# Scaling from PSUM at the start-up, with the scan and the decay moved to later places, in a fused state-space and gated feed-forward kernel

## Chip, cores, metric

One core of a Trainium2 chip. The metric is the device time of one execution in microseconds (us); lower is better. TensorE is called PE, VectorE DVE, ScalarE ACT and GpSimd POOL in the profile.

On one core "slow" means only this: more than 1.5% above the fastest execution of the same kernel. A ratio is the mean time of one kernel's fast runs over that of the other's fast runs of the same rounds, so it is not quite the ratio of the medians that are quoted. The experiments ran in four batches, on four different chips; kernels of different batches are compared through their ratio to the kernel before.

## The reference

A chunked state-space layer (4 batches, 8 heads, 768 tokens, head size 32, state size 16) feeds a gated feed-forward layer (256 to 1536 and back, on 3072 tokens):

```python
cum = np.cumsum(log_a_chunk, axis=-1)
L = np.exp(cum[..., :, None] - cum[..., None, :]) * causal
y_intra = einsum('bhij,bhjd->bhid', einsum('bhin,bhjn->bhij', C, B) * L, x)
y_inter = einsum('bhin,bhnd->bhid', C, state) * np.exp(cum)[..., None]
state   = exp(sum(log_a_chunk)) * state + sum_j(B_j x_j * exp(cum_end - cum_j))
...
out = (np.maximum(x @ w_gate, 0) * (x @ w_val)) @ w_out
```

The kernel never takes a logarithm: it forms the running product of `a` with a scan, multiplies C by it and B by its inverse. The tokens are handled in twelve pairs of chunks. Batch 0 holds pairs 0 to 2 and has its own scan (`cp0`); a long scan (`cp`) serves batches 1 to 3.

The names that the views use: `BT` and `CT` are the scaled and transposed B and C of a pair, g their product, `gs` the masked copy of g; inter multiplies C by the carried state, D multiplies `gs` by x, and both add up y, copied as `yT`. A gate/value group (`gv`) is the four matmuls that make gate and value for 128 features of 256 tokens; h is the value times the gate after its ReLU. The groups after the first are called late groups here. The decay matmuls make the factors of batches 1 to 3 from the long scan and from `pick`, a scaled selection matrix. g and the groups take their PSUM buffers from the same five banks. A warm-up is a matmul on zeros whose result nobody uses.

## The kernel before

The start-up, in program order on each engine (cuts marked):

```python
keep_warm(22)                       # 128x128 matmuls on zeros, result unused
d = factors()                       # 4 fp32 matmuls: cp0, transposed, into PSUM
decays(0)
keep_warm(8)
nc.vector.tensor_copy(wfac[:, 1], d)
nc.vector.memset(wg[0:1, 0, 0:1], 0.0)      # the first weights wait for this
weights(0, 2); weights(2, 4); weights(4, 6, (0,))      # issued by POOL
scale_wide(0, 1, V)                 # C of pair 0
nc.vector.reciprocal(wfac[:, 0, :, :, 0], wfac[:, 1, :, :, 0])
scale_wide(0, 0, V)                 # B of pair 0
transp(0, 1, False); keep_warm(4); transp(0, 0, True)
tevac(0, A_, V)
nc.vector.reciprocal(wfac[:, 0, :, :, 1:3], wfac[:, 1, :, :, 1:3])
scan(0, H)                          # the long scan
scale_wide(1, 1, P_); scale_wide(1, 0, P_); weights(4, 6, (1,))
keep_warm(6)
G_wide(0); keep_warm(7); gcopy(0, 0); gmask(0, 2, V, True); keep_warm(5, ...)
...
f0 = gvh(0, 0, 0, True)             # first gate/value group of 256 tokens
G_wide(1)
decay()                             # fp32 matmuls for batches 1 to 3
adds(1)
...
late = [gvh(0, f, 0, True) for f in (1, 2, 3)]
...
decay_factors()
...
halves(0, 1, 0, 1, 2, 3, 4, 5)
```

## Time and profile before

| | before |
|---|---|
| time, median of the first 3 runs | 124.55 us (124.37 to 124.59) |
| span of the profiled execution | 122.7 us |
| PE busy | 118.1 us, 96% |
| PE full from | 10.57 us |

The views that carry the argument on the chain are in the prediction. One more: the timeline of PE in its first 7 us. Its columns are start us, length us of the group, engine, line, operation, output and inputs, array part, and how many.

```profile
1.06 2.53 PE L189 MATMUL w<-warm 128*128 128x128 bf16 x22 [1.06 <-DVE tmask L163]
3.52 0.63 PE L217 MATMUL fac<-identf,cp 48*64 48x24 f32 x8
4.08 1.03 PE L189 MATMUL w<-warm 128*128 128x128 bf16 x8
...
5.17 0.62 PE L189 MATMUL w<-warm 128*128 128x128 bf16 x4
...
5.79 0.50 PE L189 MATMUL w<-warm 128*128 128x128 bf16 x6
6.42 0.42 PE L418 MATMUL g<-CT,BT 32*64 32x256 bf16 x16
```

See the length of a group against its count: 22 warm-ups in 2.53 us are one per 0.11 us, 6 warm-ups from 5.79 on take 0.50 us in all, with one every 0.06. From about 5.7 us PE runs at twice the rate. The slower spacing is called half rate below, the faster one full rate.

### The profile page before, as it was taken

To read this page: it belongs to the slowest core of one execution; us is meant where nothing else is said; L and a number is where in the kernel's file an instruction comes from. 1 tells how busy PE (TensorE), PEld (TensorE's weight loads), DVE (VectorE), ACT (ScalarE), POOL (GpSimd) and SP (SyncE) were. 2 spreads that over 40 slices of the span, in tenths; PEclk is the share of its full clock that TensorE was granted. 3 is DMA by queue.
4 is the path that set the end of the run, shared out by engine and by line. 5 is a ranking of instruction groups with operands and counts; after the bars stand their busy time and mean duration, and the time that the engine had idled before them with its cause. 6 is when DMAs were issued, how large, how long until landed. Compare 5 with 4: busy or idle time off the path is not lost.

```text
span 122.7 us, 3665 instructions
## 1 busy us (share of the span) xinstructions
PE 118.1 (96%) x1404; PEld 82.4 (67%) x1404; DVE 88.0 (72%) x200; ACT 76.3 (62%) x169; POOL 48.2 (39%) x108
## 2 busy tenths in 40 slices
PE   6989999999999999999999999999999999999990
PEld 6856784577875478874577864677854678844790
DVE  4798988872799864988763897855987656788410
ACT  0467688835987725786635886545877447876420
POOL 6499989361455127360351806033600033000000
DMA  3999999996979995999999498960580002200022
GB/s 63 220 208 146 171 192 194 189 172 103 115 89 139 143 142 143 103 150 205 150 114 140 154 136 138 110 117 0 189 52 0 0 0 91 85 0 0 0 91 86
DMA packets 77489, 13.93 MB, mean 113 GB/s; under 512 B 70064, under 2 KB 77472, under 8 KB 77472
## 3 DMA queue, kind: packets, MB, share of 16 engines
q1 hardware_dynamic: 70128, 10.61, 54.2%
q0 software_dynamic: 4288, 2.36, 14.1%
q10 hardware_dynamic: 3056, 0.72, 2.7%
q8 instruction: 11, 0.18, 0.6%
q14 instruction: 6, 0.05, 0.1%
HBM read 11.13 MB, written 3.15 MB: 116 GB/s over the span
## 4 chain that ended last, share of the span: by engine, by line
PE 92%; POOL 4%; DVE 1%; issue 1%; DVEq 0%
PE o L713 26%; PE gv L686 21%; PE gate L668 15%; PE val L671 15%; PE y L643 2%; PE g L548 2%; PE w L189 2%; POOL wg L199 2%; POOL bs L322 1%; PE y L632 1%; PE o L707 1%; PE A_ps L601 1%; PE g L418 1%; POOL wv L199 1%; PE y L523 1%; PE dec L262 1%
## 5 line engine op out<-in xcount | busy, mean ns | idle before, releaser
L675 DVE TENSOR_TENSOR h<-r,val 128x512 bf16<-128x512 bf16 x44 | 30.0, 685 | 7.3 <-ACT r L674 7.2
L713 PE MATMUL o<-wo,h 128*128 128x256 bf16 x276 | 33.1, 273 | 0.0
L674 ACT ACTIVATE r<-gate 128x512 bf16<-128x512 f32 x44 | 26.3, 597 | 9.7 <-PE gate L668 9.3
L713 PEld LDWEIGHTS <-h 128*128 128x128 bf16 x276 | 25.9, 98 | 5.3 <-issue 1.7
L668 PE MATMUL gate<-yT,wg 128*128 128x512 bf16 x88 | 26.2, 379 | 0.0
L671 PE MATMUL val<-yT,wv 128*128 128x512 bf16 x88 | 26.2, 379 | 0.0
L692 DVE TENSOR_TENSOR h<-r,gv 128x256 bf16<-128x256 bf16 x56 | 22.5, 419 | 2.6 <-ACT r L689 1.8
L689 ACT ACTIVATE r<-gv 128x256 bf16<-128x256 f32 x56 | 21.2, 386 | 2.3 <-PE gv L686 0.2
L686 PE MATMUL gv<-yT,wg 128*128 128x256 bf16 x112 | 21.5, 273 | 0.0
L686 PE MATMUL gv<-yT,wv 128*128 128x256 bf16 x112 | 21.4, 273 | 0.0
L556 POOL TENSOR_SCALAR_AFFINE_SELECT gs<-gs 128x512 bf16<-128x512 bf16 (+1 forms) x16 | 8.0, 523 | 30.0 <-ACT gs L567 30.0
L573 DVE TENSOR_TENSOR gs<-g,maskUT 128x512 bf16<-128x512 f32 x16 | 10.3, 685 | 11.4 <-issue 5.6
L338 POOL TENSOR_TENSOR tok<-bcr,scaleBC 128x128 bf16<-128x128 f32 x32 | 12.2, 409 | 14.1 <-DMA bcr<-in_B_dram 13.0
L671 PEld LDWEIGHTS <-wv 128*128 128x128 bf16 x88 | 8.6, 98 | 10.4
L668 PEld LDWEIGHTS <-wg 128*128 128x128 bf16 x88 | 8.6, 98 | 8.9
L686 PEld LDWEIGHTS <-wv 128*128 128x128 bf16 x112 | 11.0, 98 | 1.3
L686 PEld LDWEIGHTS <-wg 128*128 128x128 bf16 x112 | 10.2, 98 | 1.9 <-DVE yT L536 0.2
L567 ACT CAST gs<-g 128x512 bf16<-128x512 f32 x8 | 4.7, 589 | 6.7 <-PE g L548 6.7
L656 ACT CAST yT<-y 128x512 bf16<-128x512 f32 x8 | 4.7, 586 | 5.1 <-PE y L643 2.5
L433 DVE TENSOR_TENSOR gs<-g,wmask 128x512 bf16<-128x512 f32 x9 | 5.9, 680 | 2.6 <-PE g L418 2.6
L189 PE MATMUL w<-warm 128*128 128x128 bf16 x49 | 5.5, 284 | 1.1 <-DVE tmask L163 1.1
L189 PEld LDWEIGHTS <-warm 128*128 128x128 bf16 x58 | 5.0, 126 | 1.7 <-DVE tmask L163 1.1
(122 smaller groups left out, 115.8 us busy)
## 6 DMA issues: line engine op xcount, KB each, us to landing
xr<-in_x_dram SPq DMA_DIRECT2D x17, 128.0 KB, 3.2
out_dram<-ob SPq DMA_DIRECT2D x3, 512.0 KB, 3.2
bcr<-in_C_dram SPq DMA_DIRECT2D x17, 64.0 KB, 2.9
bcr<-in_B_dram SPq DMA_DIRECT2D x17, 64.0 KB, 2.9
out_dram<-ob SPq DMA_DIRECT2D x4, 256.0 KB, 3.5
xr<-in_x_dram SPq DMA_DIRECT2D x3, 256.0 KB, 4.1
wo<-in_moe_w_out_dram POOLq DMA_DIRECT2D x2, 384.0 KB, 8.5
wg<-in_moe_w_gate_dram POOLq DMA_DIRECT2D x4, 128.0 KB, 4.0
```

The costliest lines, as they stand in the source:

```text
L189: nc.tensor.matmul(out=w, lhsT=warm, rhs=rhs, start=True, stop=True)
L338: eng.tensor_tensor(out=dst[:, t, j * (1 + t)], in0=src[:, j, :, t], in1=f[:, j, :, 4 * t:4 * t + 4].to_broadcast([128, 2, 4, N]), op=ALU. ...
L556: nc.gpsimd.affine_select(out=dst, in_=dst, pattern=[[0, n], [1, 128]], compare_op=ALU.is_ge, fill=0.0, base=0, channel_multiplier=-1)
L573: nc.vector.tensor_tensor(out=d[:, q], in0=g[q], in1=m, op=ALU.mult)
L668: nc.tensor.matmul(out=g, lhsT=wg[:, k, fs], rhs=yT[:, k, tk], start=(k == 0), stop=(k == 1))
L671: nc.tensor.matmul(out=v, lhsT=wv[:, k, fs], rhs=yT[:, k, tk], start=(k == 0), stop=(k == 1))
L674: nc.scalar.activation(r, g, AF.Relu)
L675: nc.vector.tensor_tensor(out=fst[b][:, f], in0=r, in1=v, op=ALU.mult)
L686: nc.tensor.matmul(out=gv_[:, j], lhsT=w[:, k, fs], rhs=yT[:, k, tk], start=(k == 0), stop=(k == 1), skip_group_check=True)
L689: nc.scalar.activation(r, gv_[:, 0], AF.Relu)
L692: nc.vector.tensor_tensor(out=fst[b][:, f, u * 256:(u + 1) * 256], in0=r, in1=gv_[:, 1], op=ALU.mult)
L713: nc.tensor.matmul(out=o[:, ts % 2], lhsT=fst[b][:, f, ts * 128:(ts + 1) * 128], rhs=wo[:, f], start=(f == 0), stop=(f == NF - 1), skip_gr ...
```

## The change

The intent: take the copy and the two reciprocals of the factors, and the long scan, out of the chain of pair 0, so that PE becomes full sooner. The inverse is taken of the scan itself, and a second set of factor matmuls brings it into PSUM, from where DVE scales. ACT makes the SBUF copies from which POOL scales the later pairs. The long scan runs in two halves in gaps of DVE, so the decay matmuls, which need it, move to a later place. The second warm-up group, eight matmuls, goes, and the others lose two each.

```diff
     load_bc(0, 0, nc.sync, nc.scalar)
+    load_x(0, nc.sync, nc.scalar)
+    load_bc(1, 1, nc.sync)
     a_sb = glob.tile([2 * BH, H], FP32)
@@ 
-    nc.vector.tensor_copy(heads, ...)
+    rc0 = glob.tile([R, 128], FP32)
+    nc.vector.reciprocal(rc0, cp0)
@@ scale_wide
-        f = wfac[:, j, :, :, p]
+        f = (fac[j] if p == 0 else wfac[:, j])[:, :, :, p]
@@ the start-up
-    keep_warm(22)
-    d = factors()
-    decays(0)
-    keep_warm(8)
-    nc.vector.tensor_copy(wfac[:, 1], d)
+    keep_warm(20)
+    fac = [None, factors(cp0)]
+    fac[0] = factors(rc0)
@@
     scale_wide(0, 1, V)
-    nc.vector.reciprocal(wfac[:, 0, :, :, 0], wfac[:, 1, :, :, 0])
+    nc.scalar.copy(out=wfac[:, 1], in_=fac[1])
     scale_wide(0, 0, V)
+    nc.scalar.copy(out=wfac[:, 0], in_=fac[0])
     transp(0, 1, False)
-    keep_warm(4)
+    keep_warm(2)
@@
-    nc.vector.reciprocal(wfac[:, 0, :, :, 1:3], wfac[:, 1, :, :, 1:3])
-    scan(0, H)
+    chunk_heads()
+    decays(0)
@@
-    keep_warm(6)
+    keep_warm(4)
@@
-    middle()
+    scan(0, H // 2)
@@
     yevac_wide(0, A_, V)
+    scan(H // 2, H)
     load_bc(2, 1, nc.sync)
@@
     cast_x(1, V)
+    middle(0)
+    middle(1)                       # pick, now on POOL
@@
     G_wide(1)
-    decay()
     adds(1)
@@
-    decay_factors()
@@
-    halves(0, 1, 0, 1, 2, 3, 4, 5)
+    halves(0, 1, 0, 1, 2)
+    decay()
+    halves(0, 1, 3)
+    decay_factors()
+    halves(0, 1, 4, 5)
```

(The two loads at the top are moved up: they stood below the load of `a_sb`. Left out: the function bodies that take an argument more, and the decay matmuls that leave out batch 0, 48 columns in place of 64.)

More of the change, by code (lines that the diff above doesn't have):

```diff
@@ L138 @@
     load_bc(0, 0, nc.sync, nc.scalar)
+    load_x(0, nc.sync, nc.scalar)
+    load_bc(1, 1, nc.sync)
     a_sb = glob.tile([2 * BH, H], FP32)
     nc.sync.dma_start(out=a_sb, in_=a.rearrange("b h (w s) -> (b h w) s", w=2))
-    load_x(0, nc.sync, nc.scalar)
-    load_bc(1, 1, nc.sync)
     load_bc(1, 0, nc.scalar)
@@ L182, with chunk_heads @@
         op0=ALU.mult, op1=ALU.add)
-    nc.vector.tensor_copy(
-        heads, oneh.rearrange("p (t q) -> p q t", t=2).to_broadcast([R, 4, 2, N]))
+    rc0 = glob.tile([R, 128], FP32)
+    nc.vector.reciprocal(rc0, cp0)
+    def chunk_heads():
+        nc.vector.tensor_copy(
+            heads, oneh.rearrange("p (t q) -> p q t", t=2).to_broadcast([R, 4, 2, N]))
     def keep_warm(n, rhs=warm):
@@ L211, with factors @@
     dec = glob.tile([128, NC], FP32)
-    def factors():
+    def factors(c):
         d = bank("fac", (128, 2, NH, PPB))
@@ L218, in factors @@
                     out=d[64 * i:64 * i + 64, r].rearrange("p h k -> p (h k)"),
-                    lhsT=cp0[:, r:128:2], rhs=idr[:, i:R:2], start=(r == 0), stop=True,
+                    lhsT=c[:, r:128:2], rhs=idr[:, i:R:2], start=(r == 0), stop=True,
                     tile_position=(0, 64 * i), skip_group_check=True)
@@ L240, in scan, with middle @@
             initial=cp[:, s0 - 1:s0] if s0 else 1.0, op0=ALU.mult, op1=ALU.add)
-    def middle():
-        nc.vector.reciprocal(rmid, cp[:, H - 1:H])
-        nc.vector.tensor_scalar_mul(pick[:, 0], pairs[:, 0], rmid)
+    def middle(step):
+        if step == 0:
+            nc.vector.reciprocal(rmid, cp[:, H - 1:H])
+            return
+        nc.gpsimd.tensor_scalar_mul(pick[:, 0], pairs[:, 0], rmid)
     fac3 = glob.tile([128, 2, 2, NH], FP32)
@@ L249, in decay @@
     def decay():
-        bank_ = mm.tile([128, HC * 2 * NB * 8 + 16], FP32, tag="tp", name="dec")
-        n = HC * 2 * NB * 8
-        d = bank_[:, 0:n].rearrange("p (k w b h) -> p k w b h", k=HC, w=2, b=NB)
-        st["dec3"] = d3 = bank_[:, n:n + 16].rearrange("p (r h) -> p r h", r=2)
+        n = HC * 2 * (NB - 1) * NH
+        bank_ = mm.tile([128, n + 2 * NH], FP32, tag="tp", name="dec")
+        d = bank_[:, 0:n].rearrange("p (k w b h) -> p k w b h", k=HC, w=2, b=NB - 1)
+        st["dec3"] = d3 = bank_[:, n:].rearrange("p (r h) -> p r h", r=2)
         for r in range(2):
@@ L262, in decay @@
             nc.tensor.matmul(
-                out=d[:, k].rearrange("p w b h -> p (w b h)"),
-                lhsT=cp[:, k * 128:(k + 1) * 128],
-                rhs=pick.rearrange("p w h -> p (w h)"),
+                out=d[:, k].rearrange("p w b h -> p w (b h)"),
+                lhsT=cp[:, k * 128:(k + 1) * 128], rhs=pick[:, :, NH:],
                 start=False, stop=True, skip_group_check=True)
@@ L274, in decay_factors @@
             nc.scalar.copy(
-                out=scaleBC[:, :, cs, 1, :].rearrange("p b k h -> p k b h"), in_=d[:, :, w])
+                out=scaleBC[:, 1:, cs, 1, :].rearrange("p b k h -> p k b h"), in_=d[:, :, w])
     def inverse(b0, b1):
```

## The prediction

Of the times of DVE in it, those for 384 and 128 elements are of the two scans, the long one and that of `cp0`; those for 16, 32 and 48 elements are of reciprocals.

> **What bounds the kernel now.** I read the page first (busy shares), then the chain of waits, then the timeline of the first 15 us. The page says that TensorE (PE) is busy nearly all the time:

> ```profile
> PE 118.1 (96%) x1404; PEld 82.4 (67%) x1404; DVE 88.0 (72%) x200; ACT 76.3 (62%) x169; POOL 48.2 (39%) x108
> PE 92%; POOL 4%; DVE 1%; issue 1%; DVEq 0%
> ```

> Busy time is no proof, but the chain that ended last says the same: 92% of it is PE. Only its start lies elsewhere. The chain in order of time (start us, length us, what):

> ```profile
> 4.34 0.09 DVE wg L773
> 4.43 0.30 DVE bs L322
> 4.73 0.93 POOL wg L199
> ...
> 8.54 1.70 POOL bs L322 x4
> ...
> 10.28 0.28 PE tpb L367 x2
> 10.57 0.11 PE w L189 x2
> 10.68 0.45 PE gv L686 x4
> 11.13 0.39 PE g L418 x16
> 11.51 0.34 PE dec L257 x8
> 11.85 0.81 PE dec L262 x6
> 12.66 0.14 PE y L458 x4
> ...
> 12.84 1.42 PE gv L686 x12
> ```

> The reader is to see two things. Until 10.57 us PE waits for the start-up (pair 0 on DVE; weight issues and the scaling of pair 1 on GpSimd). From 10.57 on, every link is PE, and so on to 119.75 us. So **the end is the moment at which PE becomes full, plus the PE work still to be done then.** A change helps only if it brings that moment forward or takes PE work away after it.

> What runs between 10.5 and 12.8 on DVE, from the timeline:

> ```profile
> 9.38 0.14 DVE L243 RECIPROCAL rmid<-cp 64x1 f32<-64x1 f32 x1
> 9.56 0.34 DVE L244 TENSOR_SCALAR pick<-identf,rmid 64x32 f32<-64x32 f32 x1
> 9.96 0.42 DVE L540 CAST yT<-Aps 128x256 bf16<-128x256 f32 x1
> 10.31 0.28 DVE L477 SCALAR_TENSOR_TENSOR T<-T,dec,Aps 128x64 f32<-128x64 f32 x1
> 10.61 0.29 DVE L392 COPY BT<-tpb 128x256 bf16<-128x256 bf16 x1
> 10.81 0.42 DVE L350 CAST xb<-xr 128x512 bf16<-128x512 f32 x1
> 11.62 0.69 DVE L433 TENSOR_TENSOR gs<-g,wmask 128x512 bf16<-128x512 f32 x1 [0.40 <-PE g L418]
> 12.23 0.41 DVE L692 TENSOR_TENSOR h<-r,gv 128x256 bf16<-128x256 bf16 x1
> ```

> After the first gate/value group of 10.68 the next can only come when the h at 12.23 has freed its bank: there are five shared banks, four hold the g of pair 1 and the fifth that group. It ends at 12.64; PE goes on at 12.84. Between lies a hole of PE, and the decay matmuls (0.34 + 0.81 = 1.15 us) fill it. **In the kernel before they are all but free.**

> [...] 384 elements took 0.89 us, or 2.3 ns each, against 685 ns for 512 of a plain tensor_tensor; 128 elements took 0.62 us, so a start cost comes on top. [...] 16, 32 and 48 elements took 246, 341 and 428 ns, about 5.7 ns per element. [...] the six loads of the wide decay matmuls took 0.74 us, 123 ns each, nearly their whole 0.81, so I give nothing for their narrowing from 64 to 48 columns.

> **The change part by part.**

> Pair 0's factors. Out of DVE's path go the copy of the factors (0.21), one reciprocal (0.25) and, later, the other (0.34). In comes a reciprocal of 48x128: 428 + 80 x 5.7 = 0.88 us, estimated. The first scan ended at 3.24, so it ends at about 4.13; the cheap memset on which GpSimd's first weights wait follows at 4.2 (4.40 before). PE runs 20 warm-ups in place of 22 (0.115 each), does the first factors at about 3.4 to 4.0, then waits for the reciprocal and does the second set at 4.2 to 4.85 (0.63 in the timeline). DVE scales C at 4.2 and B at 4.88 (before: 4.43 and 5.12). So the chain of pair 0 gains about 0.25 us, not the 0.46 of the two instructions taken off: the new reciprocal and the second factors lie in its place.

> The full scan. Before, it stood at 6.39 to 7.28 on DVE, in front of the first mask of pair 0, whose g was ready at 6.84. Now only heads (0.19) and ends (0.22) stand there, over by 6.4, and g comes at about 6.6. The first mask starts at 6.65 in place of 7.21, and the last ends at about 8.9 in place of 9.46: 0.56 gained. But the last matmuls of pair 0 also wait for x, the sums and the carried state on ScalarE, and these gain only the 0.25 to 0.3. So the y of pair 0 goes from 9.96 to about 9.65.

> Where the scan goes. Its first half fits while D is computed (8.9 to 9.45). Its second half stands between the yT copy and the carry, on the path to BT. Each half is 0.89 / 2 plus the doubled start cost, so 0.5 to 0.55. DVE then reads: yT 9.65 to 10.07, scan to 10.6, carry to 10.85, BT to 11.15, xb to 11.5, reciprocal 0.14. Before, BT was there at 10.90. **The 0.3 us gained is given back by the half scan on the same path.** Pair 1's g then ends at about 11.6 (11.51 before), its mask runs at 11.7, the h of the first group ends at about 12.7, and PE goes on at about 12.85 (before 12.84).

> GpSimd. Its five issues of 3.8 us and four scalings of 1.7 us begin 0.2 to 0.5 us sooner and end at 9.55 to 10.0 in place of 10.23. That was the released link at 10.28, but DVE comes just behind it, so it pays nothing. The pick product moves to GpSimd behind the last weights (15.45 before), well before PE wants it at about 17.

> The decay. Its 14 matmuls go from the hole into the middle of the 256-column groups. There PE is the bound: groups follow each other every 0.43 us, against 0.386 us of ScalarE and 0.419 of DVE for each. So **1.0 to 1.15 us of PE work that was hidden is now on the path**, with a hole of about 1 us left behind.

> Sum: PE becomes full at 12.85 against 12.84 (0.0), plus 1.1 for the decay, about 125.65. I shade this to 125.3, since the replay of the first 13 us, made of some 25 links, can be 0.3 off and errors towards an earlier start are as likely as not, while the decay is at most 1.15.

> **Rivals.** (1) The gain stays: if GpSimd's 10.23 rather than DVE's chain was what held pair 1, or if the half scans are short (under 0.4), late groups start 0.3 to 0.5 sooner. For it speaks that the chain runs through GpSimd, that its first issue took 0.93 (the others 0.72)[...]. Against it: BT waits for DVE, and the decay still has to be paid. With half the decay absorbed by slack on the other engines it would be near 124.2. (2) The clock: warm-up matmuls come every 0.115 us until about 5.7 us and every 0.06 after. The change drops 14 of them (22+8+4+6 become 20+2+4) and leaves small gaps at 4.0, 5.3 and 6. If full rate comes later, g, D and the first groups run at half rate: 0.3 to 1 us more, 126 to 126.5. Against it: fac and transposes fill most of the room. (3) The hole: late masks of pair 1 become the wait ahead of D at 14.6 (0.5 us of slack before); GpSimd's pick adds 0.35 to a busy queue. Either costs at most 0.3.

> **Range and chances.** Rival 1 sets the low end, 124.2; the sum 125.65 plus a part of rival 2 the high end, 126.3. Two per cent is 2.5 us: faster than 122.06 would need the decay free and over 2 us out of a start-up that has 10.6 in all; slower than 127.04 would need the full decay and a bad warm-up.

> **What would show it.** Right: the 48x128 reciprocal takes 0.8 to 0.95 us and the second factors start right after it; the first mask of pair 0 starts near 6.65; each half scan takes about 0.5; BT is copied near 11; PE stands idle between g of pair 1 and the second gate/value group, which starts at 12.6 to 13.0; the decay sits in the chain of waits at about 17 with about 1.1 us. Wrong: that group starts before 12.4, or the decay shows up beside an idle stretch, or PE has a lower rate after 6 us.

## The result

The changed kernel took 128.12 us in the median of 4 runs (127.22, 127.96 and 128.29 fast, 130.02 slow), the kernel before 124.46 in the same rounds. The ratio of the fast runs is **1.027 (95% interval 1.0212 to 1.0327): slower**; the prediction had 125.3, at most 126.3. The span of the profiled execution, a fast one, is 126.6 us against 122.7.

The page of the changed kernel: busy times, chain by engine, granted clock in 40 slices:

```profile
PE 121.4 (96%) x1392; PEld 83.7 (66%) x1398; DVE 89.1 (70%) x198; ACT 77.0 (61%) x171; POOL 48.9 (39%) x109
PE 92%; DVE 2%; DMA 1%; issue 1%; ACT 0%; DVEq 0%
PEclk9999999999999999999999999999999999999999
```

PE is as full as before and busy 3.3 us longer, though it has less to do: 14 warm-ups fewer, and 8 records of the second factor set more. (The page counts twelve fewer; six of the gate matmuls are missing from this trace, 82 of 88.) The row of the granted clock says full speed everywhere. The timeline of PE in the first 8 us says otherwise:

```profile
1.06 2.32 PE L193 MATMUL w<-warm 128*128 128x128 bf16 x20 [1.06 <-DVE tmask L163]
3.37 0.63 PE L221 MATMUL fac<-identf,cp 48*64 48x24 f32 x8
4.26 0.63 PE L221 MATMUL fac<-identf,rc 48*64 48x24 f32 x8 [0.26 <-DVE wg L776]
...
5.66 0.63 PE L193 MATMUL w<-warm 128*128 128x128 bf16 x4
6.33 0.65 PE L423 MATMUL g<-CT,BT 32*64 32x256 bf16 x16
6.92 0.93 PE L193 MATMUL w<-warm 128*128 128x128 bf16 x7
```

Hold the lines against those of before: sixteen g matmuls take 0.65 us in place of 0.42, and seven warm-ups after 6.9 us still come 0.11 us apart. PE has not left its half rate. It leaves it only at about 17.3 us, in the middle of the D matmuls of pair 1. The packed trace agrees: its list of changes of the granted clock (`0/clock` in trace.npz) begins with full rate at 17.34 us. Nothing is listed before, and the page's row counts what is before the first entry as full speed. The chain of waits (start, length, what) shows where that falls on the path:

```profile
13.19 0.58 ACT gs L442
...
13.81 2.72 PE gv L691 x12
16.53 0.33 PE y L503 x8
...
17.56 2.29 PE gv L691 x20
19.84 0.34 PE dec L263 x8
20.18 0.80 PE dec L268 x6
```

Twelve gate/value matmuls (three groups) take 2.72 us at 13.81 and would take 1.42, as the chain of before has them at 12.84; twenty at 17.56 take 2.29, 0.46 a group. The decay matmuls are on the path with 0.34 + 0.80 us.

The span grew by 3.9 us, and the two chains divide it: the late groups start at 13.81 against 12.84 (+0.97); the three groups are 1.30 longer; inter and D of pair 1 take 1.03 us against 0.68 (+0.35); the decay now comes after, not before, that start (+1.14). The sum is 3.76; 0.14 is left unassigned.

What the change did to DVE went as intended, at first. The timeline of DVE in the changed kernel:

```profile
3.26 0.94 DVE L184 RECIPROCAL rc<-cp 48x128 f32<-48x128 f32 x1
...
4.93 0.48 DVE L327 TENSOR_TENSOR bs<-bcr,fac 128x128 bf16<-128x128 f32 x2 [0.32 <-PE fac L221]
```

B of pair 0 is scaled at 4.93 (5.12 before). Of this 0.19 us, 0.09 is left where the first g starts (6.33 against 6.42), and none where it ends, at half rate (6.98 against 6.84).

### The profile page after: what moved, and what is told of

It reads as the page before. It is cut to its first block, busy times and chain, and to the rows that moved or that the text cites.

```text
span 126.6 us, 3649 instructions
## 1 busy us (share of the span) xinstructions
PE 121.4 (96%) x1392; PEld 83.7 (66%) x1398; DVE 89.1 (70%) x198; ACT 77.0 (61%) x171; POOL 48.9 (39%) x109
## 3 DMA queue, kind: packets, MB, share of 16 engines
q1 hardware_dynamic: 70128, 10.61, 54.6%
HBM read 11.13 MB, written 3.15 MB: 113 GB/s over the span
## 4 chain that ended last, share of the span: by engine, by line
PE 92%; DVE 2%; DMA 1%; issue 1%; ACT 0%; DVEq 0%
PE o L718 25%; PE gv L691 22%; PE val L676 16%; PE gate L673 14%; PE y L648 2%; PE g L553 2%; PE w L193 2%; PE g L423 2%; DMA a<-in_a_dram 1%; PE y L528 1%; PE y L637 1%; PE o L712 1%; PE A_ps L606 1%; PE dec L268 1%; PE Aps L503 1%
## 5 line engine op out<-in xcount | busy, mean ns | idle before, releaser
L673 PE MATMUL gate<-yT,wg 128*128 128x512 bf16 x82 | 24.9, 379 | 0.0
L691 PE MATMUL gv<-yT,wg 128*128 128x256 bf16 x112 | 22.5, 283 | 0.4 <-ACT gs L442 0.4
L691 PE MATMUL gv<-yT,wv 128*128 128x256 bf16 x112 | 22.4, 283 | 0.0
L691 PEld LDWEIGHTS <-wg 128*128 128x128 bf16 x112 | 10.5, 100 | 2.8 <-issue 0.4
L358 POOL CAST xb<-xr 128x512 bf16<-128x512 f32 x8 | 4.9, 610 | 2.6 <-DMA xr<-in_x_dram 1.6
L619 DVE TENSOR_TENSOR Sm<-A_ps,smask 128x256 bf16<-128x256 f32 x15 | 5.7, 416 | 0.0
```

Source lines behind the costliest of these rows:

```text
L673: nc.tensor.matmul(out=g, lhsT=wg[:, k, fs], rhs=yT[:, k, tk], start=(k == 0), stop=(k == 1))
L691: nc.tensor.matmul(out=gv_[:, j], lhsT=w[:, k, fs], rhs=yT[:, k, tk], start=(k == 0), stop=(k == 1), skip_group_check=True)
```

## The experiments

The theory: **PE's full rate has to be earned by full-size matmuls early on, and the change took them away** (14 warm-ups less, and a second set of small fp32 matmuls in their place). Rivals: the dependencies of the change (long reciprocal, half scan on the path to BT), the late decay, the later loads. "Full rate from" is of the profiled execution of each run: read from its matmul records in the kernel before and f3, whose traces list no change of the clock, and from that list in all others, where it fits the records.

| run | ratio to before, fast runs (95%) | all runs, us (slow in brackets) | full rate from, us |
|---|---|---|---|
| before (first rounds) | 1 | 124.37 to 124.59 | 5.7 |
| changed kernel | 1.027 (1.0212 to 1.0327) | 127.22, 127.96, 128.29 (130.02) | 17.3 |
| e1_after_warm | 1.0267 (1.0198 to 1.0336) | 127.56, 127.61, 128.12, 129.29 | 13.0 |
| e2_before_fewwarm | 1.0323 (1.0273 to 1.0373) | 128.27, 128.61, 128.71, 129.22 | 17.9 |
| e3_after_decayback | 1.0114 (1.0051 to 1.0178) | 125.91, 126.57 (128.51, 128.6) | 12.6 |
| e4_before_decaylate | 1.0056 (1.0017 to 1.0094) | 125.39, 125.39, 125.46, 125.8 | 5.4 |
| e5_before_fac2 | 1.0076 (1.0007 to 1.0146) | 125.3, 126.29, 126.6 (129.62) | 9.1 |
| e6_before_gap | 0.9968 (0.9897 to 1.0039) | 124.37, 125.04 (126.45, 126.48) | 8.5 |
| e7_scan_decay_only | 1.0034 (0.9992 to 1.0076) | 125.42, 125.48, 125.61, 125.63 | 6.1 |
| e8_factors_only | 1.0094 (1.0026 to 1.0162) | 126.05, 126.06, 126.51 (128.69, 129.99) | 18.9 (a slow run was traced) |
| f5_before_late48 | 1.0207 (1.0174 to 1.0239) | 126.64, 127.22, 127.41, 127.59 | before the factors |
| f4_after_late48 | 1.0349 (1.0311 to 1.0388) | 128.41, 129.17, 129.38 (131.06) | before the factors |
| f6_factors_late48 | 1.0176 (1.0139 to 1.0213) | 126.48, 126.62, 127.39 (132.05) | before the factors |
| f3_psum_c | 1.0084 (1.0039 to 1.0128) | 124.29, 124.7, 125.19, 125.79 (126.27, 126.43) | 5.5 |
| g1_late48_loads | 1.0179 (1.0121 to 1.0236) | 126.83, 127.31, 127.35, 127.35 | before the factors |
| g2_late48_decayback | 1.0363 (1.0284 to 1.0443) | 128.82, 129.73, 130.0 (130.81) | before the factors, lost again |
| g3_late48_both | 1.0214 (1.012 to 1.0308) | 127.21, 128.09 (129.3, 130.09) | before the factors, lost again (a slow run was traced) |
| g4_before_smallwarm | none given | 125.34, 126.14 (129.74, 129.81) | 9.2 |

The last was too uneven. The "slow" label needs care: the traced execution of e8, with full rate only from 18.9 us, took 128.69 us against 126.05 to 126.51 of its fast ones, and was set aside by a rule that only looks at the time. Only one execution per run is traced, so that others were long for the same cause is a guess. The readings below rest on fast runs, and on traces of fast runs, unless a slow one is named.

### Warm-ups put back, and taken away from the kernel before

e1_after_warm, from the changed kernel:

```diff
-    keep_warm(20)
+    keep_warm(22)
     fac = [None, factors(cp0)]
+    keep_warm(3)
     fac[0] = factors(rc0)
+    keep_warm(2)
...  keep_warm(2) -> keep_warm(4), keep_warm(4) -> keep_warm(6)
```

> The changed kernel with its warm-up matmuls put back and its two early waits of TensorE filled (22, 3 between the two factor sets, 2 after them, then 4 and 6). Clock theory (TensorE stays at half rate until about 17 us because the start-up has too few matmuls): a 128x128 warm-up matmul falls from 314 to 219 ns by about 6 us, the gate/value groups of 256 columns come every 0.43 us from the first one on, and the time falls by 2.5 to 3 us, to about 125.0 to 125.6. Rival (the dependencies of DVE, the scan or the late decay cost it): under 0.7 us gained, 127.3 or more, though the clock is up.

A miss: the time did not move. The trace shows why. First, the cure of the clock largely failed. PE's timeline in this run:

```profile
4.51 0.63 PE L221 MATMUL fac<-identf,rc 48*64 48x24 f32 x8
...
8.46 0.71 PE L193 MATMUL w<-gs,warm 128*128 128x128 bf16 x5
...
34.38 0.42 PE L423 MATMUL g<-turned 32*64 32x256 bf16 x16 [0.80 <-DMA turned<-tok]
```

Five warm-ups at 8.46 still take 0.71 us; full rate came at 13.0. PE had hardly an idle moment from 1.06 to 8.4 us, so mere occupation was not enough here. Second, 13.0 is still 4.3 us sooner than in the changed kernel, and PE reached the groups after pair 1 1.04 us sooner (16.45 against 17.49). The last line shows where that went: PE waits 0.80 us for the transposed tokens of pair 3, a wait that the changed kernel does not have. So an earlier full rate alone does not bring back all that was lost here; the late loads, below, take a part.

e2_before_fewwarm, from the kernel before, with nothing else touched:

```diff
-    keep_warm(22) ... keep_warm(8) ... keep_warm(4) ... keep_warm(6)
+    keep_warm(20) ...              ... keep_warm(2) ... keep_warm(4)
```

> The kernel before with nothing changed but the number of warm-up matmuls, which is that of the changed kernel (22, 8, 4, 6 become 20, 0, 2, 4). Clock theory: full rate comes several us later, and the time rises by 1.5 to 3 us, to 126 to 127.5. Rival: warm-ups sit in idle time of TensorE, so nothing changes, 124.2 to 124.7.

14 unused matmuls removed, 3.2% lost, some 4 us: no less than the change itself loses (the intervals overlap), and more than the 1.5 to 3 us that I gave it. PE's timeline:

```profile
3.38 0.62 PE L217 MATMUL fac<-identf,cp 48*64 48x24 f32 x8
4.84 0.39 PE L367 MATMUL tp<-ident,bs 128*128 128x128 bf16 x2 [0.83 <-DVE bs L322]
...
6.98 0.93 PE L189 MATMUL w<-warm 128*128 128x128 bf16 x7
```

The 0.83 us of idle stand where the eight warm-ups were, and at 6.98 the rate is the half one. This shows that the warm-up counts of the change are enough to cause the loss.

### What counts towards the rate

e5_before_fac2, from the kernel before: five of the eight warm-ups give way to a second factor set. e6_before_gap: they give way to nothing. g4_before_smallwarm: all eight stay, but use 32 rows by 64 columns of the array.

```diff
 e5:  -    keep_warm(8)
      +    factors()
      +    keep_warm(3)
 e6:  -    keep_warm(8)
      +    keep_warm(3)
 g4:  -    keep_warm(8)
      +    keep_warm_small(8)    # lhsT=warm[0:32, 0:64], rhs=warm[0:32], same 128 columns moved
```

> The kernel before, but five of its eight second warm-ups give way to a second set of factor matmuls (result unused), which takes about the same 0.6 us of TensorE. So TensorE is as busy in time as before, with other work. If only full-size matmuls count towards the rate: full rate comes several us later (314 ns warm-ups beyond 7 us) and the time rises by 2 to 3.5 us, to 126.5 to 128.5. If any busy time counts: 124.4 to 125.2 as before.

> The kernel before with eight second warm-ups cut to three and nothing in their place: 0.55 us of idle TensorE at about 4.4 us. If the rate depends on how full the first windows are of full-size matmuls, this is as bad as the run with a second factor set: 126.5 to 128.5. If a gap of half a us does no harm, 124.4 to 125.2, and only the sum of all warm-ups taken out mattered.

> The kernel before, with its eight second warm-ups made small: 32 rows by 64 columns of the array, the same 128 moving columns and so about the same time. If the used part of the array counts towards the rate, this is like cutting them (the run with a gap: some executions at 125 and some at 126.5): full rate beyond 8 us, 125.2 to 126.6. If busy time counts, as before: 124.4 to 125.2 and full rate by 6.2 us.

All three delayed full rate, to 9.1, 8.5 and 9.2 us, in fast traced runs. So a set of factor matmuls did not do the work of the five warm-ups that it stood in for, and neither did eight matmuls that kept PE just as long but used 32x64 of its array in place of 128x128. The timeline of g4 has the same 1.05 us at 4.08 as the kernel before, and half rate 4 us later:

```profile
4.08 1.05 PE L194 MATMUL w<-warm 32*64 32x128 bf16 x8
...
8.24 0.71 PE L189 MATMUL w<-gs,warm 128*128 128x128 bf16 x5
```

The times agree less well than the traces. e5 lost 0.8%, e6 nothing clear, less than I expected of both, and e6 and g4 scatter by 2 and 4.5 us. A place on the grid that differs from run to run would give such a scatter, but only one execution of each was traced.

### The parts of the change

e8_factors_only is the kernel before with the first part (factors, ACT copies, warm-ups 20, 0, 2, 4). e7_scan_decay_only is the changed kernel with just that part undone. e4_before_decaylate moves only the decay in the kernel before. e3_after_decayback puts the decay back in the changed one:

```diff
 e4, from before:                              e3, from changed:
      G_wide(1)                                     G_wide(1)
 -    decay()                                  +    decay()
      adds(1)                                       adds(1)
 ...  decay() after halves(0, 1, 0, 1, 2)      ...  halves(0, 1, 0, 1, 2, 3, 4, 5)
                                               ...  pick on nc.vector
```

> The kernel before with only the first part of the change: inverses of the scan, two factor sets read from PSUM, copies on ScalarE, warm-ups 20, 0, 2, 4, heads and ends behind the transposes; scan, loads and decay as before. Clock theory: half rate to beyond 9 us; the decay is in its hole, so 126.3 to 128. Rival (this part gains what was intended, 0.25 us, and the loss lies in the rest): 124.1 to 124.5.

> The changed kernel with its first part undone: factors copied and inverted on DVE as before, 22, 8, 4 and 6 warm-ups; the split scan, the order of the loads, pick on GpSimd and the late decay stay. Clock theory: full rate by about 6 us and the time is that of the late decay alone, 125.0 to 125.7. Rival (split scan and late loads of pair 2 add to it): 126 to 127.

> The kernel before with nothing but the decay matmuls and their copies moved into the 256-column groups, as in the change. If the decay filled a hole that stays open: 124.5 + 1.0 to 1.15 = 125.5 to 125.7. If the groups of before only queued behind the decay (they wait for a ScalarE copy that ends at 12.1, not for the product at 12.6) they move up by 0.5 to 0.7 and the cost is 0.4 to 0.7: 124.9 to 125.2. Clock theory: full rate at 5.7 us as before.

> The changed kernel with the decay matmuls and their copies put back where they were (between g and the sums of pair 1) and the pick product back on DVE; warm-ups as changed. If the late decay costs what its records say (1.15 us) and fills the hole here: 126.9 to 127.3, the clock still late. If the clock alone is at fault: 127.8 to 128.3. If the matmuls of the decay raise the activity enough to bring full rate earlier, more, 126.0 to 126.5.

With its warm-ups and one factor set, the changed kernel is at 125.5 us (e7), within a few tenths of what the late decay alone gives (e4), and it repeats within 0.2 us. So scan, loads and pick cost next to nothing as they stand there, and the big loss sits in the first part. e8 has that part alone, and lost 0.9% in its three fast runs, at the lower end of what I expected or below (126.3 to 128). With the 0.6% of e4 this makes 1.5%, not 2.7. Its two other runs, 128.69 and 129.99, are set aside as slow; the first of them was traced, and has full rate only from 18.9 us. So the fast runs of e8 may leave out the very ones in which the rate came late; the size of the first part's loss is better taken from e7.

The late decay costs 0.56%, 0.7 us, not 1.1. One line of e4's timeline of PE tells why:

```profile
12.13 0.38 PE L686 MATMUL gv<-yT,wg 128*128 128x256 bf16 x2 [0.50 <-ACT gs L437]
```

The first late group starts at 12.13, not 12.78 as before, and what it waits for is the ACT copy of pair 1's g, not DVE's product. In the kernel before it was only queued behind the decay.

e3 gained 1.6%, more than the decay can give, and full rate came at 12.6 us there; which of the two it was, its two fast runs cannot tell.

### The change with full rate given

48 warm-ups ahead of the factors in place of 22 or 20 push the start-up back (first factor matmul at 5.1 to 6.1 us in place of 3.4 or 3.5), but by then PE is at full rate in every traced run (from 3.8 to 5.8 us). f5 is the kernel before so treated, f4 the changed kernel, f6 the first part alone.

```diff
-    keep_warm(20)      # 22 in the kernel before
+    keep_warm(48)
```

> Control for the next two: the kernel before with 48 warm-ups ahead of the factor matmuls in place of 22. The start-up is pushed back by about 2.2 to 2.6 us, and full rate has come by the time the factors are ready. If TensorE's start is what counts and the clock is up in both: 124.5 plus the delay, 126.7 to 127.2. Its spread from run to run should be small if the spread comes from the moment of full rate.

> The changed kernel with 48 warm-ups in place of 20, so that its start-up comes 2.2 to 2.6 us later but at full rate. Clock theory: the delay costs nothing or less than nothing, for what it costs is got back by the rate: 127.0 to 127.9, against 127.2 to 128.3 without it; and against the kernel before with the same 48 it loses only the late decay, less what the chain gains: 0 to 0.8 us. Rival (the dependencies of the change cost 3 us): 129.5 to 131.

> The first part of the change alone (two factor sets read from PSUM), with 48 warm-ups. With the clock up in both, this measures the part by itself: against the kernel before with 48 it should be 0.1 to 0.4 us faster, 126.4 to 126.9, if the intent holds; equal or slower if the long reciprocal eats the gain.

f6 against f5: 1.0176 against 1.0207, 0.4 us in favour of the first part, of the size intended (the intervals overlap, so this is likely, not sure). The traces agree: from the first factor matmul to the first gate matmul of 512 tokens f6 takes 14.42 us (5.26 to 19.68), f5 14.68 (5.43 to 20.11). f5's own runs spread over 0.95 us, no less than those of the kernel before in the same rounds (0.83), against what I expected.

f4 was a miss: at full rate the changed kernel still loses 1.4% to f5. Its late groups start 8.0 us after the factors (6.00 to 13.99), against 9.1 us in f5 (5.43 to 14.52), so they come 1.1 us sooner, about what the decay takes later. Not all of this is a shorter chain: in f5 the decay still stands ahead of these groups, and moving it alone brought them forward by 0.65 us in e4 (12.78 to 12.13). Where is the rest? The spans of the two traced runs are 126.7 and 124.9 us. Of these 1.8 us, 0.57 lie ahead of the factors, since full rate came later in the traced run of f4 (5.6 against 4.4 us). More lies in the g of pair 3:

```profile
34.66 0.42 PE L423 MATMUL g<-turned 32*64 32x256 bf16 x16 [0.94 <-DMA turned<-tok]
```

PE waits 0.94 us there for the transposed tokens of pair 3. f5 waits there too, for 0.37 us (and f6 for 0.74), so this is 0.57 of the difference. From the factors to the first gate matmul of 512 tokens, with the decay between them, f4 takes 0.37 us more than f5 (15.05 against 14.68); some 0.3 is left. Behind the wait of 0.94 us stands a chain of POOL work that starts with the scaling of pair 2, and this waits for its loads: C issued at 12.48 was used at 19.85, B issued at 12.89 at 22.93. In the kernel before the loads went out at 10.44 and 10.85, and POOL used them at 15.45 without a wait on either. The load is released by a one-element memset that now stands behind the half scan. Its start is not all: in f5 the same loads went out at 12.18 and 12.59, hardly sooner than in f4, and landed within 5.8 us, against 7.3 and 10.0 in f4. What slowed them there, the weight loads ahead of them for one, was not tested.

g1 moves these loads ahead of the second half scan, g2 puts the decay back, g3 does both:

```diff
 g1:       yevac_wide(0, A_, V)
      +    load_bc(2, 1, nc.sync)
      +    load_bc(2, 0, nc.sync)
           scan(H // 2, H)
      -    load_bc(2, 1, nc.sync)
      -    load_bc(2, 0, nc.sync)
```

> The changed kernel with 48 warm-ups and the loads of pair 2 issued ahead of the second half scan in place of behind it (some 0.5 us sooner). If the late loads of pair 2 are what made TensorE wait 0.9 us for the turned tokens of pair 3, that wait falls to under 0.5 us: ratio to the kernel before 1.029 to 1.032 in place of 1.035. If the loads are slow for the weights[...] and not for their start, no change: 1.033 to 1.037.

> The changed kernel with 48 warm-ups and the decay back between g and the sums of pair 1, pick on DVE. The first late group waits for a ScalarE copy 0.9 us after g, so 0.6 to 0.9 of the 1.15 us is hidden again: ratio 1.027 to 1.031. If the decay there delays the late groups by its full length, no gain, 1.034 or more.

> Both at once. If the two are the whole difference from the kernel before with 48 warm-ups (1.0207), this comes to 1.016 to 1.024, that is, at equal rate and without these two the change is neutral or a little faster. If 1.028 or more, another cost is still missing.

g1 gained 1.7 points, more than I gave it: 1.0179, level with f5 (1.0207) and f6. C was used at 15.73, B at 17.65, and the wait for pair 3's tokens fell, in its timeline of PE, to 0.54 (I had said under 0.5):

```profile
33.10 0.42 PE L423 MATMUL g<-turned 32*64 32x256 bf16 x16 [0.54 <-DMA turned<-tok]
```

So at equal rate, with loads in time, the change is worth about nothing: what the chain gains, the late decay spends (g1 takes 15.04 us from the factors to that gate matmul). Of the 1.6 us between the spans of the traced runs of f4 and g1 (126.7 and 125.1) the shorter wait explains 0.40; full rate came earlier in that of g1 (3.8 against 5.6 us, its factors at 5.14, those of f4 at 6.00), which explains another 0.86; some 0.3 is open.

g2 was a miss, and a lesson. The decay back in its place gained nothing (1.0363 against 1.0349 of f4), since pick, on DVE behind the half scan and the cast, is late. g3 came out inside the range that I gave it, but on two fast runs, with an interval that reaches into both of its answers; the trace of one of its slow runs shows what that of g2 shows. The timeline of PE in g2, a fast run:

```profile
14.34 0.41 PE L263 MATMUL dec<-pick,cp 64*64 64x8 f32 x8 [0.69 <-DVE pick L250]
14.68 0.86 PE L268 MATMUL dec<-pick,cp 64*128 64x48 f32 x6
15.66 0.39 PE L691 MATMUL gv<-yT,wg 128*128 128x256 bf16 x2
...
16.57 0.63 PE L691 MATMUL gv<-yT,wv 128*128 128x256 bf16 x2
```

0.69 us idle and 1.2 us of fp32 decay matmuls, and from 16.06 to 19.47 us the rate drops back to half: two gate/value matmuls take 0.63 us in place of 0.38. This time the page's row of the granted clock shows it, with a 5 in its sixth slice.

### A version meant to beat both

f3_psum_c keeps one factor set and all warm-ups, and takes only what is cheap from the change: C scaled, and inverted, from PSUM, the copy on ACT, the weights at once.

```diff
-    d = factors()
+    st["d"] = d = factors()
-    nc.vector.tensor_copy(wfac[:, 1], d)
...
-    nc.vector.reciprocal(wfac[:, 0, :, :, 0], wfac[:, 1, :, :, 0])
+    nc.vector.reciprocal(wfac[:, 0, :, :, 0], d[:, :, :, 0])
+    nc.scalar.copy(out=wfac[:, 1], in_=d)
```

> A version meant to beat both: the kernel before with all its warm-ups and one factor set, but C of pair 0 scaled straight from PSUM, the inverse for B taken straight from PSUM, the copy to SBUF moved to ScalarE, and the first weights issued at 3.5 us. The copy (0.21 us) leaves the chain of pair 0 and GpSimd starts about 0.7 us sooner; the late groups still queue behind the decay. 124.1 to 124.4 if GpSimd and DVE both move up by 0.2 us; 124.5 or more if the early weights slow the loads of B and C, or if the moment of full rate, which this does not touch, drowns it.

Its best run, 124.29 us, is where I expected it. Its others are not: the mean of its four fast runs is 0.84% above the kernel before, and why is open, as only the best was traced. No kernel here clearly beats the kernel before.

## Why the prediction was wrong

**The step that failed is the clock.** The sum gave it nothing; it stood as rival (2), with "0.3 to 1 us more" and, against it, "fac and transposes fill most of the room". They did not: in e5 a factor set did not do the work of five warm-ups (full rate from 9.1 us in place of 5.7), and in e1 filling the gaps, with two such sets in the start-up, did not bring full rate before 13.0 us. The half rate lasted to 17.3 us, not for "the first groups" only. It cost 1.30 + 0.35 us after 13.81, by the chain. Ahead of that, the late groups start 1.40 us later than in e7 (13.81 against 12.41), which has scan, loads and decay as in the change and full rate from 6.1 us. Together some 3 us; between the traced runs of the two lie 2.7 (128.29 and 125.63). Its sign, and that it would show as "a lower rate after 6 us", were named; its size was off by about three times.

**The bank step failed too.** The prediction had the late groups wait for the h at 12.23. They wait for ACT's copy of g (e4). The hole was therefore shorter than the decay, and moving the decay costs 0.7 us, not 1.0 to 1.15. e4 and e7, with the rate in time, took 125.4 and 125.5 us, near the 125.3 predicted, but in part by luck: the late groups come sooner than it had them, and all of the decay is then paid.

**What held.** The 48x128 reciprocal took 0.94 us (0.88 predicted), the second factors started right after it at 4.26 (4.2), B was scaled 0.19 us sooner (0.24), the half scans took 0.54 and 0.60 us (0.5 to 0.55; together 0.25 more than the 0.89 of the one scan before), the decay sits in the chain with 1.14 us. The narrower wide matmuls of the decay took 0.80 us in place of 0.81, so giving nothing for them was right; but the "123 ns each" of their loads is the time of all six divided by six, and a single record is 183 to 188 ns. The first mask (7.14, not 6.65), BT (12.03, not 11.15) and the late groups (13.81, not 12.85) came late, with g and D of pair 0 at half rate.

**What was not in it.** The late loads of pair 2. In the changed kernel they are hidden, for the slow PE needs pair 3 later still: B of pair 2 was used only at 21.26 us, yet PE's g of pair 3 did not stall. They show when the rate comes sooner and the loads are still late (e1, f4). In e7 they go out at 10.90 and 11.31 and are used at 16.02 without a wait.

**What stays open.** What decides when the rate changes, beyond the few counts and sizes of matmuls tried here; why the grid lies differently in every run; what slows the loads of pair 2 in f4; 0.3 us between the traces of f4 and g1.

## What to carry to other kernels

Matmuls that look like filler may hold the clock up: before removing or replacing them, read the spacing of PE's matmuls, not its busy share or the page's row of the granted clock, which read full speed through 16 us of half rate in the changed kernel. Here fp32 ones (e5, full rate from 9.1 us in place of 5.7) and ones on 32x64 of the array (g4, from 9.2) did not do the work of those on 128x128. When a chain is shortened, ask what its waiting time was used for: here it held warm-ups and an almost free decay. And follow each transfer whose release stands behind an instruction that moves.
